# A linear attention and Fourier feed-forward kernel: its planned instruction order is kept for longer, with other priorities

## The chip, the cores and the metric

The kernel runs on one core of one Trainium2 chip. The metric is the device time of one execution in microseconds (us); less is better. The core's engines each work through a queue of their own, in order: PE (TensorE, matrix products), DVE (VectorE), ACT (ScalarE), POOL (GpSimd) and SP (SyncE, which mostly issues DMA transfers). Waits between engines go over semaphores.

## The reference

```python
# attention without softmax, per batch and head: q, k, v are (8, 8, 576, 64)
kv = np.einsum('bhsd,bhse->bhde', k, v)
out = np.einsum('bhsd,bhde->bhse', q, kv)
x = out / sqrt(mean(out**2, -1) + 1e-6) * g_norm      # then to (8, 576, 512)
# Fourier mixing and a feed-forward layer
u = x + real(fft(fft(x, axis=1), axis=2))
un = (u - mean(u)) / sqrt(var(u) + 1e-6)
y = u + maximum(un @ w_ch1, 0) @ w_ch2                # 512 -> 2048 -> 512
```

All arrays come in and go out in float32, the two weights in float64. For each of the 4608 tokens the feed-forward layer takes 2048 hidden values, in 16 slices of 128.

## The kernel before

**Stages.** For each batch of 576 tokens: `plan_kv` loads k and v and multiplies them (PE line 574); `plan_q_load` and `plan_q` load q and transpose it on PE (line 643, evicted by ACT at line 647); `plan_out` makes the attention output for three row groups t (PE line 669; ACT lines 686 and 691, DVE line 696 for the norm's sums, POOL line 709 for the gain); `plan_y` turns the sums into scales (ACT, DVE and POOL in turn); `plan_fold` scales and folds the rows into sums and differences (DVE lines 774 and 785, POOL lines 792 and 801, ACT line 798). Folding halves the Fourier transforms, which are products with cosine and sine tables: `plan_seq` along the tokens (PE line 816, ACT line 830, DVE line 834), `plan_chn` along the channels (PE line 851, ACT line 863, DVE line 871, sums on POOL at lines 883 and 886, then stores of u). `plan_turn` transposes u for the feed-forward layer (PE line 942, ACT line 951, DVE line 954). Large products are split into a high and a low part and take three passes.

The feed-forward layer works on nine blocks of 512 tokens. `plan_early` takes the first three of the 16 weight slices for a block as soon as its tokens are there: the first layer (PE line 424), the activation split on ACT and DVE (lines 434 and 437), the second layer (PE line 442), and partial sums stored to memory. `plan_w` converts float64 weights, mostly on DVE (lines 359 to 369, 986, 995). When all batches are through, a second part, written as a plain loop, does the other 13 slices.

**What sets the order in the first part.** The stages don't issue instructions at once. Each makes `Op` entries in a `Plan`, with an engine, a cost in nanoseconds, a rank (smaller goes first), the operations that it follows and the buffers it takes. `Plan.run` plays the entries through with these costs: at each simulated time an engine that is free takes, of the entries that are ready and whose buffers are free, the one of lowest rank, and only then are its instructions emitted. `rank(b, stage)` is 10 b + stage, with 40 less for batch 0; `KV, QT, OUT, SCL, FOLD, SEQ, CHN, NRM` are the stages 0 to 7; the evictions of `plan_out` have 20 less. `SHIFT` adds to the rank of a group of operations, named by stage, engine (or DMA) and rounded rank. Early feed-forward operations have ranks from 1000 on. `plan_spare` adds 45 operations of two matmuls each on a constant tile (line 494, cost 454) with the highest rank of all, ready from the plan's 12 us on: they fill time in which PE has nothing else to do, and are all emitted, so their number is fixed.

The emitted program then goes through a scheduler of the compiler, with a cost model of its own, which can reorder instructions of an engine where their dependencies allow it. `Plan.pin` keeps it from that: each instruction that is emitted up to `PIN_UNTIL` (in the plan's time, ns) gets a dependency without a semaphore on the one before it on its engine. `PINNED` lists all five engines.

```python
for i in traced[start:]:
    if i.engine not in self.pinned or now > PIN_UNTIL:
        continue
    last = self.last.get(i.engine)
```

Behind that limit the scheduler is free in its order. Matmuls on float32 operands show as two records each in the profile (lines 574 and 669): a k-v operation is 16 and 4 records, an output operation 32.

Of the kernel before, what the change touches and what calls it, by code (L numbers as in the profile page):

```python
# [46 lines left out]
SPARE_FROM = 12000  # L47


PIN_UNTIL = 95000  # L50
PINNED = {
    mybir.EngineType.PE, mybir.EngineType.DVE, mybir.EngineType.Activation,
    mybir.EngineType.Pool, mybir.EngineType.SP,
# [2 lines left out]


SHIFT = {
    ("", "POOL", 20): 18,
    ("chn", "ACT", -34): 54.5,  # L60
    ("dft", "DVE", -35): 83.5,
    ("fold", "DVE", -36): -33.5,
    ("out", "DVE", -58): 31,
    ("out", "ACT", 2): 157,
    ("q", "PE", -39): 3,
    ("q", "PE", 21): -30,
    ("q", "ACT", 31): -19.5,
    ("q_load", "DMA", -39): -1.5,
}


# [17 lines left out]
class Plan:  # L89
# [18 lines left out]
    def op(self, eng, cost, rank, emit, after=(), bufs=(), lag=0, port=False, wait=0):  # L108
        o = Op()
        o.port = port or eng == "POOL"  # L110
        o.dense = False
        o.wait = wait
        o.eng, o.cost, o.rank, o.emit, o.lag = eng, cost, rank, emit, lag
        o.after = [a for a in after if a is not None]
        o.bufs = list(dict.fromkeys(bufs))
        for b in o.bufs:
            b.left += 1
        o.n = len(self.ops)
        o.stage = emit.__qualname__.split("<locals>.")[1].split(".")[0]
        o.done, o.dma = None, False  # L120
        self.ops.append(o)
        return o
# [130 lines left out]
def kernel(  # L253
# [52 lines left out]
    op, dma = plan.op, plan.dma  # L306
# [165 lines left out]
    def rank(b, stage):  # L472
        return 10 * b + stage - (40 if b == 0 else 0)

    KV, QT, OUT, SCL, FOLD, SEQ, CHN, NRM = range(8)
# [25 lines left out]
    dft = {}  # L501
# [25 lines left out]
    def plan_kv(b):  # L527
        kvt = ring("kvt", qkv, [P, NPAIR, D], "kvt")
        ps = bank_buf("ps_k")
        mm, lds = [], []  # L530
        rest = []
        for c, src in (("k", k), ("v", v)):
            kr = Buf("kr", lambda c=c: qkv.tile([P // 2, H, D], F32, name=c + "r", tag="kr", bufs=RINGS["kr"]))
            rest.append(kr)
        for pr in range(NPAIR):
            hs = slice(2 * pr, 2 * pr + 2)
            ts = []
            ld = []
            for c, src, kr in (("k", k, rest[0]), ("v", v, rest[1])):
                on = dict(eng="ACT") if b == 0 and c == "v" else {}  # L540
                start = nc.scalar.dma_start if on else nc.sync.dma_start
                if b < 2 and pr >= NPAIR - EARLY_KV[b]:
                    main = Buf("h", lambda c=c: base.tile(
                        [P, 2, 4, D], F32, name=c + "m", tag="r", bufs=RINGS["h"]
                    ))
                else:
                    main = Buf("kv", lambda c=c: qkv.tile(
                        [P, 2, 4, D], F32, name=c + "m", tag="m", bufs=RINGS["kv"]
                    ))
                ts.append(main)  # L550
                ld.append(dma(
                    256, rank(b, KV),
                    lambda main=main, src=src, hs=hs, start=start: start(
                        main.t.rearrange("p h j d -> p h (j d)"),
                        src[b, hs, : 4 * P].rearrange("h (p j) d -> p h (j d)", j=4),
                    ),
                    bufs=[main], **on,
                ))
                if pr == 0:
                    lds.append(dma(  # L560
                        128, rank(b, KV),
                        lambda kr=kr, src=src, start=start: start(
                            kr.t, src[b, :, 4 * P :].rearrange("h p d -> p h d")
                        ),
                        bufs=[kr], **on,
                    ))

            def go(pr=pr, ts=ts):
                km, vm = ts[0].t, ts[1].t
                kr, vr = rest[0].t, rest[1].t  # L570
                for j in range(5):
                    for s in range(2):
                        h = 2 * pr + s
                        nc.tensor.matmul(  # L574
                            ps.t[s * D : (s + 1) * D, pr * D : (pr + 1) * D],
                            km[:, s, j, :] if j < 4 else kr[:, h, :],
                            vm[:, s, j, :] if j < 4 else vr[:, h, :],
                            start=(j == 0),
                            stop=(j == 4),
                        )  # L580

            mm.append(op("PE", 1080, rank(b, KV), go, ld + lds, [ps, kvt] + ts + rest))
        done = op(
            "ACT", 370, rank(b, KV),
            lambda: nc.scalar.copy(kvt.t.rearrange("p c t -> p (c t)"), ps.t[:, : NPAIR * D]),
            mm, [ps, kvt],
        )
        if b:
            return kvt, kvt, [done], ld

        kvg = ring("kvt", qkv, [P, NPAIR, D], "kvt")

        def gain():
            nc.vector.tensor_tensor(
                kvg.t, ps.t[:, : NPAIR * D].rearrange("p (c t) -> p c t", c=NPAIR),
                gb.unsqueeze(1).to_broadcast([P, NPAIR, D]), ALU.mult,
            )

        scaled = op("DVE", 330, rank(b, KV), gain, mm + [i_gb], [ps, kvg])
        return kvt, kvg, [done, scaled], ld  # L600
# [30 lines left out]
    def plan_q(b, side, j, qt, ld):  # L631

        n = TR + 1 if side == 0 and j == 0 else TR
        fq = ring("fq", qkv, [P, NPAIR, TR + 1], "fq")
        done = []
        ps = bank_buf("ps_q")

        def view():
            return ps.t[:, : NPAIR * n].rearrange("p (c t) -> p c t", c=NPAIR)

        def turn():
            for m in range(NPAIR):
                nc.tensor.transpose(view()[:, m, :], qt.t[:n, j, m * P : (m + 1) * P], ident[:n, :n])  # L643

        def take():
            dst = fq.t[:, :, :n]
            nc.scalar.copy(dst[:, :, TR - 1 :: -1] if side else dst, view())  # L647

        tr = op("PE", 330, rank(b, QT), turn, ld, [qt, ps, fq])
        done.append(op("ACT", 490, rank(b, QT), take, [tr], [ps, fq]))  # L650
        if side and j == 2:
            done.append(op(
                "POOL", 100, rank(b, QT), lambda: nc.gpsimd.memset(fq.t[:, :, TR:], 0.0), [tr], [fq]
            ))
        return fq, done
# [151 lines left out]
    def plan_seq(b, grp, xs, pt, dones):  # L807
        part, ch = divmod(grp, 2)
        ps = bank_buf("ps_f")

        def mm():
            idx = 0
            for t in range(3):
                n = rows[t]
                for a, c in passes:
                    nc.tensor.matmul(  # L816
                        ps.t[:, :NS],
                        xs[t].t[a][:n, part, ch * P : (ch + 1) * P],
                        cs[:n, part, c, t, :],
                        start=(idx == 0),  # L820
                        stop=(idx == 8),
                    )
                    idx += 1

        r = rank(b, SEQ)
        a = op("PE", 1200, r, mm, dones + [dft["s", part]], [ps, pt] + xs)
        a.dense = True
        h = op(
            "ACT", 414, r - D2,
            lambda: nc.scalar.activation(pt.t[0][:, part, ch, :], ps.t[:, :NS], AF.Copy), [a], [ps, pt],  # L830
        )

        def low():
            nc.vector.tensor_tensor(
                pt.t[1][:, part, ch, :], ps.t[:, :NS], pt.t[0][:, part, ch, :].bitcast(F32), ALU.subtract
            )

        return op("DVE", 450, r - D2, low, [h], [ps, pt])
# [78 lines left out]
    def plan_turn(b, side, t, x, done):  # L917
# [15 lines left out]
        ps = bank_buf("ps_t")  # L933
        blocks = [unTs[j] for j in dict.fromkeys(p[0] for p in pieces)]
# [7 lines left out]
                nc.tensor.transpose(view()[:, c, :], x.t[:n, at : at + P], ident[:n, :n])  # L942

        r = rank(b, NRM)
        a = op("PE", 330, r, turn, done, [x, ps] + blocks)
        for j, lo, hi, at, step in pieces:
            stop = at + step * (hi - lo - 1) + (1 if step > 0 else -1)
            to = slice(at, None if stop < 0 else stop, step)
# [121 lines left out]
    for b in range(B):  # L1070
        kvt, kvg, kvt_done, kv_loaded = plan_kv(b)
# [4 lines left out]
        xs = [ring("x", one, [P, 2 * DM], "x") for _ in range(3)]  # L1076
# [4 lines left out]
        for side in range(2):  # L1081
            qt, loaded = plan_q_load(b, side)
# [25 lines left out]
        pt = Buf("pt", lambda: [one.tile([P, 2, 2, NS], F32R, name=f"pt{i}") for i in range(2)])  # L1108
# [39 lines left out]
    r = rank(B, 5)  # L1148
    a = op("DVE", 300, r, p0_in, zeros)
    a = op("PE", 1200, r, p0_mm, [a], [ps0])  # L1150
    a = op("DVE", 900, r, p0_out, [a], [ps0, p0t, p0u])
# [86 lines left out]
    blocks = early[::-1][: len(early) - 2] + early[:2] + list(range(1, NBLK - NSEG)) + [0]  # L1238
# [198 lines left out]
```

## Time and profile before

| What | Value |
|---|---|
| Time, median of 3 runs | 1025.26 us (1024.71 to 1025.57) |
| Profiled execution, its own time | 1022.79 us |
| Its span | 1021.0 us |
| PE busy | 1002.3 us (98% of the span) |
| DVE, ACT, POOL busy | 475.3, 324.8, 314.4 us |

The span is the time from the first to the last instruction of the profiled execution, and the execution's own time is a little more. Rows of the profile name the line of the kernel, the engine, the operation and the tiles as `out<-in`; `x372` is the number of records. In rows of groups, busy us and mean ns follow, then the engine's idle time just before, with what ended it. In rows of stretches, the length comes first, then busy time and record count for PE, PEld (weight loads), DVE, ACT and POOL, then the granted TensorE clock (1.00 is full), the busy share of the DMA engines and GB/s. In a timeline, a start, a duration and an operation. Neighbouring matmuls overlap in the pipeline, so their durations exceed the distance between their starts.

### The profile page before, as it was taken

Reading aid. Unit: us, or ns where it says so; the run is one execution under the profiler, and the core shown is the slowest. Engines: PE = TensorE matmul, PEld = TensorE weight load, DVE = VectorE, ACT = ScalarE, POOL = GpSimd, SP = SyncE. Lnnn points to the kernel's source line nnn. Section 1 sums busy time; section 2 is a strip of 40 time slices with the busy share of each in tenths; the row PEclk is TensorE's granted clock in tenths of the full one; section 3 lists DMA queues with packets and bytes.
Section 4 is the critical chain, followed back from the end, with each engine's and each line's share of the span. In section 5 each row is a group of like instructions: output and inputs, shape, how many; then the busy total and the mean of one; then the engine's idle time right before and its main releaser. Section 6 shows DMA issues by size and latency. Waiting matters only on the chain.

```text
span 1021.0 us, 15425 instructions
## 1 busy us (share of the span) xinstructions
PE 1002.3 (98%) x6070; PEld 844.0 (83%) x6070; DVE 475.3 (47%) x847; ACT 324.8 (32%) x657; POOL 314.4 (31%) x328
## 2 busy tenths in 40 slices
PE   5999999999999999999999999999999999999997
PEld 5898888889888888888888888888888888888886
DVE  4897656654788879997131313131221311311211
ACT  2666556554644434344221202121121120210110
POOL 0526768775675132235722303020020010100000
PEclk9999999999999999999999999999999999999999
DMA  9989778664346775645553514230320400400101
GB/s 250 212 230 282 181 209 258 162 170 131 137 163 213 268 253 191 236 129 170 161 179 86 180 59 150 82 125 0 141 67 1 165 21 1 165 0 1 42 1 42
DMA packets 109260, 140.74 MB, mean 138 GB/s; under 512 B 51854, under 2 KB 76482, under 8 KB 104580
## 3 DMA queue, kind: packets, MB, share of 16 engines
q1 hardware_dynamic: 105652, 132.28, 41.9%
q0 software_dynamic: 1920, 6.29, 1.9%
q10 hardware_dynamic: 1616, 1.18, 0.5%
q8 instruction: 48, 0.79, 0.3%
q14 instruction: 24, 0.20, 0.1%
HBM read 88.33 MB, written 51.40 MB: 137 GB/s over the span
## 4 chain that ended last, share of the span: by engine, by line
PE 97%; DMA 1%; ACT 0%; POOL 0%; DVE 0%; issue 0%; SPq 0%; DVEq 0%; POOLq 0%
PE ps_h L424 38%; PE acc L442 38%; PE ps_o L669 4%; PE ps_f L816 4%; PE ps_f L851 4%; PE ps_k L574 3%; PE ps_s L494 2%; PE ps_q L643 2%; PE ps_t L942 2%; DMA qt<-in_q_dram 1%; PE ps_w L383 1%; DMA vm<-in_v_dram 0%; POOL x L883 0%; ACT x L686 0%; DVE uu L1324 0%
## 5 line engine op out<-in xcount | busy, mean ns | idle before, releaser
L424 PE MATMUL ps_h<-unTh,w 128*128 128x512 f32 x1152 | 356.6, 391 | 1.2 <-ACT fq L647 1.2
L442 PE MATMUL acc<-w,hh 128*128 128x512 f32 x1152 | 345.5, 390 | 0.0
L437 DVE SCALAR_TENSOR_TENSOR hl<-ps_h,hh 128x512 fp32r<-128x512 f32 x144 | 99.1, 688 | 371.8 <-ACT hh L434 367.5
L442 PEld LDWEIGHTS acc<-w,hh 128*128 128x128 f32 x1152 | 215.1, 188 | 44.3
L424 PEld LDWEIGHTS ps_h<-unTh,w 128*128 128x128 f32 x1152 | 214.8, 188 | 44.8 <-ACT fq L647 1.4
L434 ACT ACTIVATE hh<-ps_h 128x512 fp32r<-128x512 f32 x144 | 85.8, 596 | 454.0 <-PE ps_h L424 439.2
L424 PE MATMUL ps_h<-unTl,w 128*128 128x512 f32 x576 | 224.3, 389 | 0.0
L442 PE MATMUL acc<-w,hl 128*128 128x512 f32 x576 | 213.5, 389 | 0.0
L424 PEld LDWEIGHTS ps_h<-unTl,w 128*128 128x128 f32 x576 | 108.1, 188 | 22.6
L442 PEld LDWEIGHTS acc<-w,hl 128*128 128x128 f32 x576 | 108.1, 188 | 22.6
L1271 POOL DMA_INDIRECT uu<-u_scr,rowidx x24 | 23.2, 968 | 285.1 <-DVE uu L1324 177.9
L709 POOL TENSOR_TENSOR x<-x,gb 96x512 f32<-96x512 f32 (+1 forms) x42 | 55.0, 1330 | 45.7 <-ACT x L686 40.3
L1290 POOL TENSOR_TENSOR uu<-uu,up 128x512 f32<-128x512 f32 x36 | 45.7, 1298 | 45.2 <-ACT up L1287 45.2
L1234 POOL TENSOR_TENSOR w<-wap,w 128x512 fp32r<-128x512 f32 x18 | 26.4, 1467 | 75.3 <-ACT w L1233 69.1
L669 PEld LDWEIGHTS ps_o<-kvt,fq 64*96 64x96 f32 (+1 forms) x864 | 40.9, 162 | 5.7 <-issue 4.0
L1324 DVE SCALAR_TENSOR_TENSOR uu<-acc,rs_yb,uu 128x512 f32<-128x512 f32 x36 | 25.2, 744 | 42.5 <-PE acc L442 42.5
L669 PE MATMUL ps_o<-kvt,fq 64*96 64x64 f32 (+1 forms) x864 | 44.4, 248 | 0.0
L696 DVE TENSOR_REDUCE ss<-ps_o 96x8 f32<-96x512 f32 (+1 forms) x48 | 32.0, 682 | 26.5 <-ACT ps_o L691 26.3
L792 POOL TENSOR_TENSOR xe<-ab 96x256 f32<-96x256 f32 (+1 forms) x46 | 38.0, 845 | 18.7 <-DVE ab L785 17.9
L816 PE MATMUL ps_f<-cs,xh 96*128 96x290 f32 (+1 forms) x192 | 39.0, 300 | 0.0
L1278 DVE BATCH_NORM_STATS2 bst<-uu 128x6 f32<-128x512 f32 x36 | 24.5, 687 | 29.0 <-DMA uu<-u_scr,rowidx 19.8
L851 PE MATMUL ps_f<-cd,pt 128*96 128x258 f32 (+1 forms) x288 | 37.8, 285 | 0.0
(114 smaller groups left out, 1022.4 us busy)
## 6 DMA issues: line engine op xcount, KB each, us to landing
raw<-in_moe_w_ch_dram SPq DMA_DIRECT2D x32, 512.0 KB
unT_scr<-unTh SPq DMA_DIRECT2D x9, 1024.0 KB
unT_scr<-unTl SPq DMA_DIRECT2D x9, 1024.0 KB
part_scr<-part SPq DMA_DIRECT2D x36, 256.0 KB
unTh<-unT_scr SPq DMA_DIRECT2D x9, 1024.0 KB
unTl<-unT_scr SPq DMA_DIRECT2D x9, 1024.0 KB
up<-part_scr SPq DMA_DIRECT2D x36, 256.0 KB
out_dram<-uu SPq DMA_DIRECT2D x36, 256.0 KB
```

Of the source, the lines that this page charges most:

```text
L424: nc.tensor.matmul(ps, w[c][:, kc * P : (kc + 1) * P], unT[a][:, kc, :], start=(idx == 0), stop=(idx == 3 * KC - 1),)
L434: nc.scalar.activation(hh, ps, AF.Relu)
L437: nc.vector.scalar_tensor_tensor(hl, ps, 0.0, hh.bitcast(F32), ALU.max, ALU.subtract)
L442: nc.tensor.matmul(acc, hpair[a][:, i * P : (i + 1) * P], w[c], start=(first and n == 0), stop=(last and n == 2),)
L574: nc.tensor.matmul(ps.t[s * D : (s + 1) * D, pr * D : (pr + 1) * D], km[:, s, j, :] if j < 4 else kr[:, h, :], vm[:, s, j, :] if j < 4 els ...
L669: nc.tensor.matmul(pss[s].t[:n, at : at + D], fqs[side].t[half, m, :n], kvt.t[half, m], start=True, stop=True,)
L696: nc.vector.tensor_reduce(ss.t[0][:n, :, t, s::2], pss[s].t[:n].rearrange("p (u m e) -> p u m e", u=2, e=D), AX.X, ALU.add,)
L709: nc.gpsimd.tensor_tensor(v_, v_, gb[:n].unsqueeze(1).to_broadcast([n, H, D]), ALU.mult)
L792: nc.gpsimd.tensor_tensor(o[:, s], a[:, 0], a[:, 1], ALU.subtract if s else ALU.add)
L816: nc.tensor.matmul(ps.t[:, :NS], xs[t].t[a][:n, part, ch * P : (ch + 1) * P], cs[:n, part, c, t, :], start=(idx == 0), stop=(idx == 8),)
L851: nc.tensor.matmul(ps.t[:n, :ND], pt.t[a][:, part, ch, offs[t] : offs[t] + n], cd[:, part, c, ch, :], start=(idx == 0), stop=(idx == 5),)
L1290: nc.gpsimd.tensor_tensor(us[j][i], us[j][i], part, ALU.add)
```

## The change

The limit of the pin goes from the plan's 95 us to 260 us. The table of shifts is replaced: ten entries go, thirteen come. Four PE costs in the plan change. The new entries, by what they touch: the load of the token order; batch 3's stores of u, its norm sums on DVE and its gain on POOL; batch 2's fold on POOL; batch 0's loads of k and v, its query loads (two of the three row groups), its query copies on ACT and its output evictions on ACT; batch 4's output on PE; batch 2's query transposes on PE (to a lower rank, so earlier); the first weight slice on ACT and the third on DVE. The shifts that stood before are dropped where no new entry repeats them.

```diff
@@ -47,7 +47,7 @@
 SPARE_FROM = 12000
 
 
-PIN_UNTIL = 95000
+PIN_UNTIL = 260000
 PINNED = {
     mybir.EngineType.PE, mybir.EngineType.DVE, mybir.EngineType.Activation,
     mybir.EngineType.Pool, mybir.EngineType.SP,
@@ -56,16 +56,19 @@
 
 
 SHIFT = {
-    ("", "POOL", 20): 18,
-    ("chn", "ACT", -34): 54.5,
-    ("dft", "DVE", -35): 83.5,
-    ("fold", "DVE", -36): -33.5,
-    ("out", "DVE", -58): 31,
-    ("out", "ACT", 2): 157,
-    ("q", "PE", -39): 3,
-    ("q", "PE", 21): -30,
-    ("q", "ACT", 31): -19.5,
-    ("q_load", "DMA", -39): -1.5,
+    ("", "DMA", 20): 6,
+    ("chn", "DMA", 36): 166,
+    ("fold", "POOL", 24): 26.5,
+    ("kv", "DMA", -40): 3,
+    ("out", "ACT", -58): 54.5,
+    ("out", "DVE", 12): 169,
+    ("out", "POOL", 32): 53.5,
+    ("out", "PE", 42): 113.5,
+    ("q", "ACT", -39): 43,
+    ("q", "PE", 21): -38,
+    ("q_load", "DMA", -39): 7.5,
+    ("w", "ACT", -60): 43,
+    ("w", "DVE", 6): 158.5,
 }
 
 
@@ -579,7 +582,7 @@
                             stop=(j == 4),
                         )
 
-            mm.append(op("PE", 1080, rank(b, KV), go, ld + lds, [ps, kvt] + ts + rest))
+            mm.append(op("PE", 980, rank(b, KV), go, ld + lds, [ps, kvt] + ts + rest))
         done = op(
             "ACT", 370, rank(b, KV),
             lambda: nc.scalar.copy(kvt.t.rearrange("p c t -> p (c t)"), ps.t[:, : NPAIR * D]),
@@ -646,7 +649,7 @@
             dst = fq.t[:, :, :n]
             nc.scalar.copy(dst[:, :, TR - 1 :: -1] if side else dst, view())
 
-        tr = op("PE", 330, rank(b, QT), turn, ld, [qt, ps, fq])
+        tr = op("PE", 378, rank(b, QT), turn, ld, [qt, ps, fq])
         done.append(op("ACT", 490, rank(b, QT), take, [tr], [ps, fq]))
         if side and j == 2:
             done.append(op(
@@ -823,7 +826,7 @@
                     idx += 1
 
         r = rank(b, SEQ)
-        a = op("PE", 1200, r, mm, dones + [dft["s", part]], [ps, pt] + xs)
+        a = op("PE", 1250, r, mm, dones + [dft["s", part]], [ps, pt] + xs)
         a.dense = True
         h = op(
             "ACT", 414, r - D2,
@@ -942,7 +945,7 @@
                 nc.tensor.transpose(view()[:, c, :], x.t[:n, at : at + P], ident[:n, :n])
 
         r = rank(b, NRM)
-        a = op("PE", 330, r, turn, done, [x, ps] + blocks)
+        a = op("PE", 360, r, turn, done, [x, ps] + blocks)
         for j, lo, hi, at, step in pieces:
             stop = at + step * (hi - lo - 1) + (1 if step > 0 else -1)
             to = slice(at, None if stop < 0 else stop, step)
```

No other line changes: the instructions, their operands and the buffers are those of before.

## The prediction

> **What bounds the kernel now.** I read the page's first line, then a table of busy time by stretch, then the waits of PE (TensorE's matmul side), and last PE's timeline and its groups inside the stretch that the change touches.
>
> ```profile
> span 1021.0 us, 15425 instructions
> ```
>
> Busy time of each engine by stretch of the span (first columns: stretch, its length, PE busy):
>
> ```profile
> 0.00:25.00 25.00, 14.64 (x150) 12.33 (x152) 10.95 (x20) 6.05 (x11) 0.96 (x9) 1.00 1.06 250
> 25.00:95.00 70.00, 70.00 (x833) 60.10 (x831) 60.08 (x103) 42.07 (x93) 28.31 (x41) 1.00 0.93 242
> 95.00:225.00 130.00, 127.02 (x1335) 110.93 (x1332) 78.23 (x143) 77.12 (x180) 96.30 (x107) 1.00 0.76 203
> ...
> 260.00:330.00 70.00, 70.00 (x463) 61.35 (x462) 57.47 (x103) 37.98 (x85) 46.65 (x48) 1.00 0.46 161
> ```
>
> PE is busy for the whole of the second and the fourth stretch. It is the only engine that is: DVE, the next one, has 60.08 of 70 us and 57.47 of 70. The one place after the start where PE shows idle time is 95 to 225 us, 130 - 127.02 = 2.98 us. The granted clock is 1.00 in every row, so no row speaks of a slow TensorE. The kernel is a queue of PE work, and a new order can only save what PE loses between its instructions: open idle time, and matmuls that start later than they could while the row still counts PE as busy.
>
> At the start PE waits for its first load, and that is a row of the waits view:
>
> ```profile
> PE ps_q L643 <- DMA qt<-in_q_dram: 10.4, 1, 10.4
> ```
>
> **How large the loss is in 95 to 225 us.** A busy share of 98% hides late starts, so I price the work of that stretch by what the same work takes in the part that is pinned now. PE's timeline there (start, duration, operation; the distance between two starts is what a piece really took):
>
> ```profile
> 53.31 0.54 PE L816 MATMUL ps_f<-cs,xh 97*128 97x290 f32 x2
> ...
> 58.24 0.82 PE L643 MATMUL ps_q<-ident,qt 96*128 96x96 f32 x8
> ...
> 59.87 1.57 PE L669 MATMUL ps_o<-kvt,fq 64*96 64x64 f32 x32
> 61.37 4.55 PE L851 MATMUL ps_f<-cd,pt 128*97 128x258 f32 x36
> 65.76 0.82 PE L643 MATMUL ps_q<-ident,qt 96*128 96x96 f32 x8
> 66.52 0.69 PE L574 MATMUL ps_k<-vm,km 128*64 128x64 f32 x16
> 67.13 0.33 PE L574 MATMUL ps_k<-vr,kr 64*64 64x64 f32 x4
> 67.39 1.16 PE L383 MATMUL ps_w<-wa,mean_t 128*128 128x128 f32 x8
> 68.39 0.83 PE L942 MATMUL ps_t<-ident,x 97*128 97x97 f32 x8
> 69.15 0.69 PE L574 MATMUL ps_k<-vm,km 128*64 128x64 f32 x16
> ...
> 77.20 0.63 PE L424 MATMUL ps_h<-unTh,w 128*128 128x512 f32 x2
> ...
> 82.77 0.69 PE L574 MATMUL ps_k<-vm,km 128*64 128x64 f32 x16
> ...
> 115.26 0.57 PE L574 MATMUL ps_k<-vm,km 128*64 128x64 f32 x12
> 115.75 0.55 PE L942 MATMUL ps_t<-ident,x 97*128 97x97 f32 x4
> ...
> 120.94 0.88 PE L942 MATMUL ps_t<-ident,x 96*128 96x96 f32 x8
> ```
>
> In the pinned part operations are whole. A sequence transform (four groups of 9, line 816) takes 58.24 - 53.31 = 4.93 us, an attention output (line 669, 32 records) 1.50, a channel transform (line 851, 36 records) 4.39, two query transposes of four (line 643) 0.76, one k-v operation (line 574, 16 and 4 records) 0.87, two output transposes (line 942) 0.76, and two first-layer operations (line 424, 24 records between 77.20 and 82.77) 5.57. From 115.26 us they are not whole: a k-v operation breaks off after 12 of its 16 records, four transposes go between, and so on until 120.94. Those 5.68 us hold 15 rows with three k-v operations, three output transposes and two query transposes, which by the prices above take 3 x 0.87 + 5 x 0.38 = 4.51 us; 1.2 us is lost there.
>
> The work of the stretch, as the groups of PE between 95 and 225 us count it:
>
> ```profile
> L669 PE MATMUL ps_o<-kvt,fq 64*96 64x64 f32 (+1 forms) x372 | 20.3, 249 | 0.0
> L851 PE MATMUL ps_f<-cd,pt 128*96 128x258 f32 (+1 forms) x144 | 19.8, 288 | 0.0
> L816 PE MATMUL ps_f<-cs,xh 96*128 96x290 f32 (+1 forms) x96 | 19.7, 300 | 0.0
> L442 PE MATMUL acc<-w,hh 128*128 128x512 f32 x48 | 15.5, 403 | 0.0
> L424 PE MATMUL ps_h<-unTh,w 128*128 128x512 f32 x48 | 15.4, 402 | 1.2 <-ACT fq L647 1.2
> L574 PE MATMUL ps_k<-vm,km 128*64 128x64 f32 x288 | 14.5, 230 | 1.0 <-DMA vm<-in_v_dram 1.0
> ...
> L643 PE MATMUL ps_q<-ident,qt 96*128 96x96 f32 (+1 forms) x99 | 11.4, 250 | 0.3
> L942 PE MATMUL ps_t<-ident,x 96*128 96x96 f32 (+2 forms) x72 | 9.5, 254 | 0.4 <-POOL x L883 0.4
> ```
>
> Attention output 372 / 32 = 11.6 operations x 1.50 = 17.4; channel 144 / 36 = 4 x 4.39 = 17.6; sequence 96 / 24 = 4 x 4.93 = 19.7 (24 of the 36 records read xh); first layer 48 / 8 = 6 x 2.785 = 16.7; second layer 48 / 6 = 8 groups of 9 matmuls of the same size, at three quarters of 2.785, 16.7; k-v 288 / 16 = 18 x 0.87 = 15.7; query transposes 99 / 4 x 0.38 = 9.4; output transposes 18 x 0.38 = 6.8. The sum is 120.0 us in a stretch of 130. So 10.0 us is lost: 3.0 open idle time (ACT 1.2, a load of v 1.0, POOL 0.4, the rest small) and 7.0 in splits and late starts that the busy column hides. This is the ceiling of the change in this stretch.
>
> **The change, part by part.** No instruction of the computation is added or taken away. PE's work is the same to the record, the 45 filler operations of line 494 with it, since the plan only ends when all are emitted; a plan with less idle time moves them to later and doesn't drop them.
>
> *The pin to 260000.* Each engine's instructions now follow the plan up to its 260 us instead of its 95 us. The plan's clock isn't the trace's: the first split piece lies at 115.75 us, so the old limit falls at or shortly ahead of that, and the new one may fall near 280. The whole stretch in which PE loses time comes under it. Two terms follow. Splits and late starts, 7.0 us: an operation's matmuls follow one another, as in 25 to 95, so between nothing and all of it is recovered. Open idle time, 3.0 us: again between nothing and all, as the order decides. I take half of each, 3.5 + 1.5 = 5.0 us. All of it is what the pinned rows show (70.00 busy of 70), but those 70 us were cushioned by filler, whose row in the groups of 25 to 95 is
>
> ```profile
> L494 PE MATMUL ps_s<-still 128*128 128x512 f32 x64 | 18.2, 413 | 0.0
> ```
>
> and the later stretch has no such cushion, only first- and second-layer operations as the thing to do meanwhile. The middle is an estimate.
>
> *The price of pinning.* It adds dependencies only within an engine, and they cost nothing in themselves. What is queued behind a waiting instruction now waits too. On PE that is the next operation, even if its operands have lain ready; on ACT and DVE the evictions that free PSUM banks; on POOL the fold and output sums; on SP every load behind a store that waits for its data. Bounds: nothing, as in 25 to 95, up to the rival below. It is not added to the sum a second time, since half of the recovery is already withheld.
>
> *The thirteen priorities.* They change the order alone. Three touch the start: the first batch's query loads go from ahead of the k loads to behind them, apart from the two for the third row group; its query copies and weight clears on ACT drop behind others. PE's first wait is for a query load, and by the ranks a query load is still the first after the weight loads, so the 10.4 us stays; I cost it at nothing. Should the first batch's chain be slowed all the same, nothing covers it, because the filler is a fixed number; bounds 0 and +3.0 us, the open idle time that PE met in the later stretch when inputs came late. The conversion of the third weight slice on DVE drops behind the batches' own work; the early first-layer operations need it, and what hides its delay is filler until that is used up. Batch 3's norm reductions, its gain multiply and its stores, batch 4's attention output and batch 2's fold on POOL move later; what hides them is the other batches' work on the same engines, as PE's four full transforms in 130 us show. Half the gain withheld stands for these too. The filler itself may run in longer or shorter pieces: 18.2 / 64 = 0.284 us each against 2.785 / 12 = 0.232 in a long run, 90 records, at most 4.7 us less if all ran together, and none if they stay scattered; I take none.
>
> *The plan's costs* (k-v 1080 to 980, transposes 330 to 378 and 360, sequence 1200 to 1250). They shape the order only. The rows above have a k-v operation at 0.87 us, nearer the new 0.98 than the old 1.08, and a sequence operation at 4.93 / 4 = 1.23, near the new 1.25; for transposes 0.38 in a pair, the new figure for queries. I give the better costs no microseconds of their own.
>
> **The sum.** The profiled execution took 1022.79 us, its span 1021.0 and 1.79 around it. 1022.79 - 5.0 = 1017.8. The median of the runs shown is 2.47 us above the profiled execution, 1025.26, and the forecast is for that: 1025.26 - 5.0 = **1020.3 us**. With the whole 10.0 us it is 1015.3.
>
> **The rivals.** *First: a late input stops a full queue.* With the pin, PE stands at an operation whose input is late while ready work lies behind it. The place is the fold, which goes from DVE to POOL, ACT and POOL again before the sequence transform can start; POOL is busy 96.30 of 130 us in that stretch, its highest share, and a DMA load has already stopped PE there for 1.0. For it: the three waits on the rows above are of just this kind (ACT 1.2, DMA 1.0, POOL 0.4; mean 0.87). Against it: 25 to 95 runs pinned without one. Price: four and a half batches between 95 and 260, three folds each, 13 places x 0.87 = 11.3 us, less about 3.5 for splits that do go away: 1025.3 + 7.8 = 1033.1 us. It decides from about 6 such stops on, since 6 x 0.87 = 5.2 us uses up the 3.5 and 2 us more. The Trainium skill, TensorE: Matmul & The Clock Gate, section "Measured speedup vs the span model", says that matmuls run strictly in program order; by that rule nothing on PE softens a bad order, and the trace agrees, with PE idle 1.2 us at one first-layer matmul while later work stood queued. The same page, section "What's actually happening", has an idle time of about 3.4 us or more halve the clock until a window of work has passed; no wait after the start here is that long, and the granted clock stays 1.00.
>
> *Second: the gain is given back.* PE reaches 260 us sooner with the same DVE work behind it (57.47 of 70 us in 260 to 330), and then waits for weight conversions or evictions. That it is never idle there now, at 82% DVE, speaks against; that 5 us is a third of DVE's 12.5 us of free time speaks for. The time is 1025 us.
>
> *Third: the order hardly changes.* The scheduler may have kept nearly the plan's order anyway, and the splits be the smaller part of the 7.0, the rest being real late inputs that any order has. Then only the 1.2 us of the one split cluster goes: 1024 us.
>
> **How the numbers follow.** A measurement of this kernel can tell 0.2%, about 2 us, from no change. Forecast 0.57; stops 0.25; gain given back 0.11; order hardly changed 0.07. The forecast's own range is 1015.3 to 1023.2, which is all faster by over 2 us; the second and third rivals lie within 2 us. So faster 0.57, same 0.18, slower 0.25. The range goes from 1014.5, just under the full recovery, with a little of the filler's 4.7, to 1032; it holds the middle rivals and most of the first; left out are the worse half of the stops and a gain past the ceiling.
>
> **What would show it.** In the profile after: the filler's and the sums' record counts are the same; between 95 and 225 us k-v operations come as 16 and 4 records without transposes between; the same work by the prices above takes 120 to 127 us there; open idle time of PE after the start is under 2 us; the first wait stays at 10 to 11 us. The forecast is wrong if PE shows waits of 0.5 us and more for POOL, ACT or loads at the folds, adding up to over 6 us; if idle time appears ahead of the first first-layer operation; or if the saved time returns as waits for DVE between 260 and 400 us.

## The result, and the profile after

The changed kernel takes 1018.33 us in the median of 5 runs (1016.90 to 1019.72), the kernel before 1025.26 (1024.71 to 1027.99). The ratio is 0.9929, with a 95% interval of 0.9912 to 0.9946: 0.5 to 0.9% faster. The profiled execution took 1016.90 us with a span of 1015.1, against 1022.79 and 1021.0 before. The forecast was 1020.3 us in a range of 1014.5 to 1032.

The table of busy time by stretch, of the changed kernel (stretch, length, then busy time and records of PE, PEld, DVE, ACT, POOL, then the granted clock):

```profile
0.00:25.00 25.00, 12.83 (x144) 10.49 (x146) 11.05 (x20) 6.06 (x11) 0.96 (x9) 1.00 0.99 234
25.00:95.00 70.00, 69.59 (x835) 60.32 (x833) 60.93 (x102) 43.64 (x93) 28.61 (x40) 1.00 0.93 240
95.00:225.00 130.00, 130.00 (x1377) 115.40 (x1373) 79.86 (x148) 80.71 (x186) 97.92 (x110) 1.00 0.79 221
225.00:260.00 35.00, 33.85 (x280) 30.07 (x279) 18.28 (x35) 19.45 (x44) 22.03 (x24) 1.00 0.34 125
260.00:330.00 70.00, 70.00 (x443) 61.73 (x443) 56.18 (x106) 35.25 (x82) 41.46 (x45) 1.00 0.44 153
```

PE's open idle time between 95 and 225 us, 2.98 us before, is gone, and 42 more records pass in that stretch, 10 of them filler. The waits of PE in the whole span:

```profile
PE ps_q L646 <- DMA qt<-in_q_dram: 12.2, 1, 12.2
PE ps_o L672 <- ACT fq L650: 1.1, 1, 1.1
PE ps_q L646 <- issue: 0.4, 1, 0.4
```

The three waits of before behind the start have made room for one of 1.1 us, at 253 us. The first wait has grown from 10.4 to 12.2 us.

PE's groups between 95 and 225 us (lines are three further on than before; rows that aren't needed are left out):

```profile
L445 PE MATMUL acc<-w,hh 128*128 128x512 f32 x66 | 21.5, 406 | 0.0
L819 PE MATMUL ps_f<-cs,xh 96*128 96x290 f32 (+1 forms) x96 | 19.7, 300 | 0.0
L854 PE MATMUL ps_f<-cd,pt 128*96 128x258 f32 (+1 forms) x144 | 18.4, 283 | 0.0
L672 PE MATMUL ps_o<-kvt,fq 64*96 64x64 f32 (+1 forms) x352 | 17.4, 248 | 0.0
L427 PE MATMUL ps_h<-unTh,w 128*128 128x512 f32 x51 | 16.1, 395 | 0.0
...
L577 PE MATMUL ps_k<-vm,km 128*64 128x64 f32 x300 | 12.9, 228 | 0.0
L646 PE MATMUL ps_q<-ident,qt 96*128 96x96 f32 (+1 forms) x104 | 11.6, 249 | 0.0
...
L945 PE MATMUL ps_t<-ident,x 96*128 96x96 f32 (+2 forms) x72 | 7.9, 249 | 0.0
...
L497 PE MATMUL ps_s<-still 128*128 128x512 f32 x10 | 3.1, 410 | 0.0
```

At the prediction's prices this is 11 x 2.09 + 4 x 4.93 + 4 x 4.39 + 11 x 1.50 + 6.4 x 2.785 + 18.75 x 0.87 + 26 x 0.38 + 18 x 0.38 = 127.6 us of work in 130, and 10 filler records at 0.284 us take the other 2.8 (the last 0.4 is the error of the prices). Nothing else is lost. Why shows in the timeline: 15 rows for three k-v operations and five groups of transposes have become whole operations.

```profile
118.45 0.88 PE L945 MATMUL ps_t<-ident,x 97*128 97x97 f32 x8
119.26 0.69 PE L577 MATMUL ps_k<-vm,km 128*64 128x64 f32 x16
119.88 0.33 PE L577 MATMUL ps_k<-vr,kr 64*64 64x64 f32 x4
120.14 0.69 PE L577 MATMUL ps_k<-vm,km 128*64 128x64 f32 x16
120.76 0.33 PE L577 MATMUL ps_k<-vr,kr 64*64 64x64 f32 x4
121.02 0.88 PE L945 MATMUL ps_t<-ident,x 96*128 96x96 f32 x8
```

To set all runs side by side I use one figure, the **loss** of a stretch: its length less PE's records in it at those prices (for a part of an operation, its share; first- and second-layer matmuls at 2.785 / 12, and the few of lines 383 and 1131 at 0.11). Filler counts as loss and is given beside it, at 0.284 us each. All in us, of the profiled executions:

| Kernel | 0 to 95 us | 95 to 225 (filler in it) | 225 to 260 | 260 to 330 |
|---|---|---|---|---|
| before | 34.0 | 10.2 (0) | 0.3 | -0.9 |
| changed | 33.7 | 2.9 (2.8) | 0.9 | -0.3 |
| changed, a second execution | 34.2 | 2.8 (2.8) | 2.5 | -0.2 |

The 7.3 us between 95 and 225, less 0.6 and 0.6 behind them, come to 6.1 us, near the 5.9 us between the spans. So the first wait's 1.8 us is not lost within the first 95 us: less filler ran there, and its rest ran behind, where it takes the 2.8 us. The second execution shows how far one program's figures differ.

### The profile page after: what moved, and what is told of

Its sections match the earlier page's. It is cut to its first block, busy times and chain, and to the rows that moved or that the text cites. A ratio compares the mean times of both kernels' runs of the same rounds, so it can differ in the third digit from the quotient of the medians.

```text
span 1015.1 us, 15417 instructions
## 1 busy us (share of the span) xinstructions
PE 996.0 (98%) x6070; PEld 840.5 (83%) x6070; DVE 470.8 (46%) x847; ACT 328.2 (32%) x657; POOL 308.8 (30%) x328
## 4 chain that ended last, share of the span: by engine, by line
PE 98%; DMA 1%; ACT 0%; issue 0%; DVE 0%; SPq 0%; DVEq 0%; ACTq 0%
PE acc L445 39%; PE ps_h L427 39%; PE ps_o L672 4%; PE ps_f L819 4%; PE ps_f L854 3%; PE ps_k L577 3%; PE ps_s L497 2%; PE ps_q L646 2%; PE ps_t L945 2%; DMA qt<-in_q_dram 1%; PE ps_w L386 1%; DVE uu L1327 0%; PE ps_o L1134 0%; ACT x L689 0%; SPq L352 0%
## 5 line engine op out<-in xcount | busy, mean ns | idle before, releaser
L1237 POOL TENSOR_TENSOR w<-wap,w 128x512 fp32r<-128x512 f32 x18 | 23.2, 1291 | 70.4 <-ACT w L1236 70.4
```

## The experiments

The theory at the outset was that the pin does it, by keeping PE's operations whole. The rival was that the new priorities do it. Each run was set beside the kernel before on the same chip; ratios are to that, with 95% intervals.

**The pin alone.** On the kernel before:

```diff
-PIN_UNTIL = 95000
+PIN_UNTIL = 260000
```

> The kernel before with the pin's limit at 260 us and nothing else changed. Theory one (the pin does it, by keeping PE's operations whole): most of the 10 us lost between 95 and 225 us goes, the start stays at a first wait of 10.4 us, so 1016 to 1020 us. Theory two (the new priorities do it, and the old order pinned would stall): 1023 to 1030 us, with waits of PE of 0.5 us and more beyond 110 us that add up to 5 us or more.

Measured: 1016.22 us, ratio 0.9919 (0.9901 to 0.9938). The loss in 95 to 225 us is 2.0 (filler 0.6); PE's first wait is 10.2 us. One number, with the old order, brings as much as the whole change. The stretch's row:

```profile
95.00:225.00 130.00, 129.09 (x1369) 114.62 (x1368) 76.49 (x146) 81.25 (x187) 103.16 (x114) 1.00 0.81 217
```

The rival's stalls did not come: PE's waits behind the start add up to 2.1 us.

**The priorities and plan costs alone.** On the changed kernel:

```diff
-PIN_UNTIL = 260000
+PIN_UNTIL = 95000
```

> The changed kernel with the pin's limit back at 95 us; priorities and plan costs stay. Theory one (the pin): the splits and late starts return behind about 115 us, and the start's first wait is 12.2 us instead of 10.4, so 1024 to 1028 us. Theory two (the priorities): 1017 to 1021 us.

Measured: 1036.51 us, ratio 1.0120 (1.0097 to 1.0143), slower than either theory had it. Two waits of PE and a row of the stretches:

```profile
PE ps_k L577 <- DMA vm<-in_v_dram: 3.7, 2, 3.1
PE ps_f L819 <- POOL xl L804: 2.9, 1, 2.9
```

```profile
135.00:140.00 5.00, 5.00 (x34) 4.26 (x31) 0.00 (x0) 0.85 (x2) 2.93 (x5) 0.50 0.98 319
```

The loss in 95 to 225 us is 15.2 us. PE waited 3.1 us up to 134.7 us, and the granted clock of the next 5 us is 0.50. The rival falls; the theory missed that these priorities, with the new plan costs, do harm without the pin.

**The pin and the costs, with the old priorities.** The changed kernel with the ten entries of before in `SHIFT`.

> The changed kernel with the ten old priorities; pin and new plan costs stay. Theory one (the pin): as the pin alone, 1016 to 1020 us, the four costs being worth under 2 us either way. Rival (the corrected costs make the pinned order fit the chip): 3 us or more faster than the pin alone.

Measured: 1016.26 us, ratio 0.9916 (0.9897 to 0.9935), next to the pin alone. The loss in 95 to 225 us is 2.1. The costs are worth nothing that can be seen here.

**The first batch's loads in their old order.** On the changed kernel:

```diff
-    ("kv", "DMA", -40): 3,
-    ("q_load", "DMA", -39): 7.5,
+    ("q_load", "DMA", -39): -1.5,
```

> The changed kernel with the first batch's loads in the old order: its query loads ahead of its k and v loads. Theory one (the start cost 1.8 us and nothing covers it): the first wait goes from 12.2 back to 10.4 us and the time from 1018.3 to about 1016.5 us. Rival (the filler's fixed number covers it, since PE has nothing real to do there): the first wait is shorter and the time stays within 1 us of 1018.3, or rises because the later order was fitted to the later start.

Measured: 1034.87 us, ratio 1.0105 (1.0082 to 1.0127): neither. The first wait did shorten, to 10.7 us, but two entries of thirteen cost 16 us. The loss is 37.2 us by 95 us, then 6.4, 4.1 and 5.9. Behind the start, the longest wait of PE and the stretch after it are

```profile
PE ps_h L426 <- DVE w L997: 3.3, 1, 3.3
```

```profile
95.00:100.00 5.00, 4.34 (x15) 3.06 (x17) 3.13 (x4) 1.26 (x3) 4.29 (x5) 0.67 0.94 286
```

It is a first-layer operation that waits for the third weight slice, whose conversion the change had put behind the batches' work on DVE; here the filler had run out at 77.3 us (at 114.8 in the changed kernel).

**The changed kernel again,** beside the next three.

> The changed kernel once more, to stand beside the next three on one chip, and beside the pin alone (ratio 0.992 to the kernel before). Theory one (the pin does it, the priorities are worth nothing or cost a little by the later start): ratio 0.992 to 0.995, so 1017 to 1020 us. If the priorities help: under 0.990.

Measured: 1018.75 us, ratio 0.9950 (0.9931 to 0.9969). With the first measurement, the change is worth 0.3 to 0.9%. The pin alone and the pin with the costs are 2 us ahead in the medians, but the intervals touch; I don't call the priorities harmful on this. Nor is it shown that the later start is free: the kernels with a first wait of 9.8 to 10.2 us (these two, and the two at the end of this section) have ratios of 0.9912 to 0.9919, the changed kernel, with 12.2 us, 0.9929 and 0.9950.

**The pin on PE alone, and on all but PE.** The set `PINNED` of the changed kernel cut to PE, and without PE.

> The changed kernel with the pin (to 260 us) on PE alone; the other four engines are left to the scheduler. Theory one in its narrow form (whole operations on PE are the gain): 1017 to 1021 us. Rival (the order of the other queues, evictions, folds and loads, sets when PE's inputs come): PE waits of over 1 us appear, and the time is 1025 us or more.

> The changed kernel with the pin on the other four engines and PE left to the scheduler. Narrow theory (whole operations on PE): splits return, 6 to 10 us more than the changed kernel, 1024 to 1029 us. Rival (the other queues' order): within 2 us of the changed kernel.

Measured: 1035.35 us, ratio 1.0107 (1.0089 to 1.0124), and 1029.76, ratio 1.0055 (1.0034 to 1.0076). Both also took pins away from the first 95 us, which the kernel before had, and there much of the time went. The row of 25 to 95 us of the first and of the second:

```profile
25.00:95.00 70.00, 65.03 (x691) 55.72 (x688) 49.86 (x89) 36.10 (x79) 19.11 (x31) 0.93 0.83 214
```

```profile
25.00:95.00 70.00, 67.63 (x779) 59.36 (x778) 55.20 (x95) 37.59 (x82) 21.30 (x29) 0.95 0.75 198
```

PE is idle for 5.0 and 2.4 us there, and the clock is not full. By 95 us the loss is 43.5 and 45.2 us, against 34.2 in the changed kernel beside them. With the pin on PE alone, PE's records stand in the changed kernel's order, by tile and shape, up to 280 us, and it is still 16.6 us slower: what it loses, it loses to the other queues' order. How much of that is behind 95 us these two kernels can't say; two further ones below keep the pins of the first 95 us.

**The pin to the end of the first part.**

```diff
-PIN_UNTIL = 260000
+PIN_UNTIL = 1000000
```

> The changed kernel with the pin over the whole of the first part. Theory one: behind the plan's 260 us little is lost any more, since PE has early feed-forward work enough there and is idle for 1.1 us at most; within 1.5 us of the changed kernel. Rival (each further pinned stretch pays like 95 to 225 us did, 10 us in 130): 3 to 5 us faster. Second rival (a late input stops the full queue): slower by 3 us or more, with waits of PE behind 260 us.

Measured: 1022.61 us, ratio 0.9976 (0.9959 to 0.9993), 3.9 us more than the changed kernel beside it. Waits of PE that the changed kernel doesn't have:

```profile
PE ps_w L386 <- POOL wp L382: 1.0, 1, 1.0
PE ps_f L819 <- ACT xh L801: 0.9, 1, 0.9
PE ps_f L819 <- POOL xl L804: 0.8, 1, 0.8
PE ps_w L386 <- DVE wap L377: 0.5, 1, 0.5
```

The loss in 260 to 330 us is 2.9 us against -0.3. This is the prediction's first rival, a late input that stops a full queue, in the part where the pin was new. PE's own order is the changed kernel's up to 280 us by tile and shape; ACT, DVE and POOL leave it at 259 to 267 us. The longer pin also takes away something useful: two weight loads that the scheduler issues at 63 and 84 us in the changed kernel come at 262 us here. Whether the waits at line 386, which are for converted weights, follow from that was not tested.

**From 95 us on, PE alone pinned; and all but PE.** On the changed kernel, in `Plan.pin` (the second the other way round):

```diff
-            if i.engine not in self.pinned or now > PIN_UNTIL:
+            until = PIN_UNTIL if i.engine == mybir.EngineType.PE else 95000
+            if i.engine not in self.pinned or now > until:
```

> The changed kernel; all engines pinned to the plan's 95 us, from there to 260 us PE alone. Narrow theory (whole operations on PE are the gain): 1017 to 1021 us. Wider theory (the gain is that all queues follow one order; PE's order with other queues rearranged brings late inputs): 1024 to 1035 us, with the start to 95 us like the changed kernel's and waits of PE for ACT, DVE or POOL behind it.

> The changed kernel; all engines pinned to the plan's 95 us, from there to 260 us all but PE. Narrow theory: splits and late starts come back, 1024 to 1029 us. Wider theory: the splits alone cost 0.1 to 0.2 us each, a few us in all, 1020 to 1025 us, since the inputs still come in the plan's order.

Measured: 1028.18 us, ratio 1.0036 (1.0022 to 1.0051), and 1022.52, ratio 0.9979 (0.9965 to 0.9993). With PE alone pinned, its records stand in the changed kernel's order up to 280 us (the other queues leave theirs at 93 to 108 us), its operations are whole, and it waits, here in its row and its timeline (its lines are one further on):

```profile
95.00:225.00 130.00, 126.17 (x1324) 111.61 (x1323) 79.15 (x143) 75.58 (x178) 92.24 (x104) 0.99 0.72 209
```

```profile
109.28 0.40 PE L820 MATMUL ps_f<-cs,xl 96*128 96x290 f32 x1 [1.67 <-POOL xl L805]
...
127.26 0.72 PE L946 MATMUL ps_t<-ident,x 96*128 96x96 f32 x6 [0.39 <-POOL x L890]
...
150.33 0.74 PE L428 MATMUL ps_h<-unTh,w 128*128 128x512 f32 x2 [1.59 <-DVE ss L700]
```

With all but PE pinned, the other queues keep the changed kernel's order beyond 225 us and PE leaves it at 79 us. The open idle time is small, 0.54 us from 95 to 225, and the splits are back:

```profile
119.12 2.47 PE L673 MATMUL ps_o<-kvt,fq 64*96 64x64 f32 x32
121.53 0.55 PE L946 MATMUL ps_t<-ident,x 97*128 97x97 f32 x4
122.01 0.33 PE L578 MATMUL ps_k<-vm,km 128*64 128x64 f32 x2
122.27 0.55 PE L946 MATMUL ps_t<-ident,x 97*128 97x97 f32 x4
122.75 0.68 PE L578 MATMUL ps_k<-vm,km 128*64 128x64 f32 x14
```

The losses of 95 to 225 us without filler are 6.6 us with PE alone, 5.2 with all but PE, 0.1 with all (and 15.2 with none, in the run of the priorities alone). The narrow theory falls and the wider one stands: with these priorities the order has to be held on PE and on the other queues together. Which of the other four matters, and whether the old priorities behave alike, was not tested.

**The start's loads and the third weight back.** The run of 1034.87 us, less one more entry:

```diff
-    ("w", "DVE", 6): 158.5,
```

> The run with the first batch's loads in the old order (1034.9 us, ratio 1.0105), and the third weight slice's conversion on DVE at its old priority too. If that conversion's delay is what that run lost its time to (PE waited 3.3 us for it at 95 us): the wait is gone and the time is 1028 us or less, 6.6 us or more of the 16 back by the wait and the halved clock behind it. Rival (that order is bad at many places, and this wait is one of them): over 1030 us, with new waits.

Measured: 1015.39 us, ratio 0.9913 (0.9895 to 0.9931). The one entry is worth 19.5 us in that order. PE's first wait is 9.8 us, and behind it PE waits once, for 0.6 us. Its row:

```profile
95.00:225.00 130.00, 129.37 (x1356) 114.51 (x1355) 79.85 (x146) 77.97 (x179) 96.78 (x108) 1.00 0.80 222
```

The loss in 95 to 225 us is 1.4, and no filler is left by then. It is the lowest median of all, but its interval overlaps those of the pin alone and of the changed kernel's first measurement. The direct price of the wait, 3.3 us and some 5 us at a clock of 0.67, is under half of the 19.5; the waits near 230 and 300 us went too. How one entry at 80 us reaches those was not traced further than that the plan gives another order.

**Less filler.** The pin and costs with the old priorities, and `SPARE = 30` for 45. It leaves out a third of the matmuls on the constant tile, which no output uses.

> The pin and the new costs with the old priorities (1016.3 us, ratio 0.9916), with 30 filler operations instead of 45. If the filler's number is a fixed cost (0.5 us each): 7 us faster, 1009 to 1011 us. Rival (the filler only runs where PE has nothing to do): the same within 1.5 us, with PE's idle time up by about 7 us. Second rival (the idle time that replaces it halves the clock): slower by 3 us or more.

Measured: 1016.07 us, ratio 0.9912 (0.9890 to 0.9933), the same as with 45. PE's row of 25 to 95 us and its longest wait behind the start:

```profile
25.00:95.00 70.00, 67.03 (x837) 58.07 (x838) 59.14 (x104) 42.53 (x94) 28.36 (x42) 0.98 0.88 235
```

```profile
PE ps_w L383 <- DVE wa L986: 2.1, 1, 2.1
```

PE is idle for 3.0 us where it wasn't, the loss by 95 us falls by only 0.2 us, from 33.3 to 33.1, and 95 to 225 us loses 4.3 instead of 2.1. The filler's number is no cost here; it fills time that is lost either way. The second rival's clock did come (0.57 from 50 to 54 us, behind the wait of 2.1 us), but the time doesn't show it.

## Why the prediction was right, and where it was not

**The bound and the ceiling** held. PE's queue is what is shortened, and the stretch named, 95 to 225 us, is where the time came from. The price list gave 10.0 us of loss there; the changed kernel loses 2.9, of which 2.8 is filler.

**The term that was mis-sized** is the recovery. The prediction took half of it, 3.5 of 7.0 us of splits and late starts and 1.5 of 3.0 us of open idle time. Both went nearly whole: operations are unbroken, and PE is busy for 130.00 of 130 us. Of the table's 10.2, 7.3 show as net gain, because 2.8 us of filler moved in. The span's gain was 5.9 us and the medians' 6.9, against 5.0. The reason given for withholding half was that the later stretch lacks filler as a cushion. The pin alone, with 0.6 us of filler there, lost no more than 2.0 us, so the cushion wasn't needed.

**The mechanism** was put partly wrong. The prediction put the gain down to whole operations on PE and counted the pins on the other queues only as a risk. With these priorities, the stretch loses 15.2 us without the longer pin, 6.6 with PE alone pinned, 5.2 with all but PE, and 0.1 with all. So PE's own order is worth 5.1 to 8.6 us and the other queues' order 6.5 to 10.0, by which is added first: inputs that come in the order PE expects are at least as large a part as whole operations.

**The start** was called unchanged, on the ground that a query load is still the first after the weight loads. It isn't. SP's issues before (start, duration, transfer):

```profile
0.74 0.99 SPq L349 DMA_DIRECT2D raw<-in_moe_w_ch_dram  x2
1.77 0.43 SPq L610 DMA_DIRECT2D qt<-in_q_dram  x1
```

and in the changed kernel:

```profile
0.74 0.99 SPq L352 DMA_DIRECT2D raw<-in_moe_w_ch_dram  x2
1.77 0.43 SPq L486 DMA_DIRECT2D gb<-in_g_norm_dram  x1
2.25 3.29 SPq L613 DMA_DIRECT2D qt<-in_q_dram  x2
```

The old shift of -1.5 had put most of the first batch's query loads at ranks of -40.5 and -40.25, ahead of the gain vector's load at -40. With the new one they are at -31.5 and -31.25, the two unshifted ones at -38.5 lead, and the gain vector's load goes first. The first query load is issued 0.5 us later and the first wait grew by 1.8 us; where the rest comes from was not traced. With the old load order the wait was 10.7 and 9.8 us. It cost nothing by 95 us; whether it costs the 2 us by which the kernels with the earlier start are ahead stays open, inside the bound of 0 to +3.0.

**The first rival,** a late input in a full queue, did not happen in the changed kernel but is real: it shows with PE alone pinned, at the fold's last POOL step that the prediction named (1.67 us for `xl`), and with the pin to the end. **The second,** a gain given back to DVE behind 260 us, did not: PE is busy for 70.00 of 70 us. **The third,** an order hardly changed, did not.

**The priorities** were costed at nothing with half the gain withheld. That the sum came out within 2 us is in part luck: the gain withheld stood for harm from the priorities, which with the pin is about 2 us in the medians. That the table is so harmless could not be known from the working. With the new costs but without the longer pin it makes the kernel 12 us slower than before, and with the pin a table that differs in two entries is 16 us worse. The third weight's conversion was named as a risk that filler hides until it is used up, and that is just where the altered table lost first.

**The signs to look for** were right on the records (90 filler records, whole k-v operations) and on open idle time under 2 us behind the start (1.1 + 0.4), and wrong on the first wait, put at 10 to 11 us.

**Smaller slips.** The plan's clock runs closer to the trace's than assumed: the order of the kernel before and that of the pin alone part at 90 us on PE and at 94 to 102 us on ACT, DVE and POOL, ahead of 115.75 us, and by the run with the pin to the end the new limit falls near 260 us rather than 280. Of DVE's 12.5 us of free time 5 us is 0.4, not a third. The first rival's own price of 1033.1 us lies above the range's end of 1032. The clock of 1.00 in the row of 0 to 25 us doesn't fit the first matmuls: the eight of line 383 at 11.03 us take 1.80 us to the next start, and the same eight at 48.57 us take 0.85. What the prediction says of program order stands in the Trainium skill, TensorE: Matmul & The Clock Gate, section "The mechanism", one section ahead of the one that it names.

## What to carry to other kernels

Price the work of a stretch by what the same operations take where they run undisturbed; a PE that shows 98% busy hid more than twice its open idle time in broken operations and late starts (7.0 against 3.0 us). When a static order is held against a scheduler that would change it, hold it on every queue or expect late inputs, and find where to stop by trying it. A table of priorities is one piece: a part of it, tried on another order, says little about what that part is worth.

## What the hardware did that was not expected

Behind a short wait of PE the clock can be halved, and need not be. The changed kernel's wait of 1.15 us, up to 254.3 and 254.8 us, stands in both of its profiled executions. The stretch behind it, in the first and in the second:

```profile
256.00:260.00 4.00, 4.00 (x19) 3.32 (x18) 3.97 (x7) 2.81 (x6) 4.00 (x4) 1.00 0.17 66
```

```profile
256.00:260.00 4.00, 4.00 (x12) 3.13 (x11) 3.96 (x7) 2.49 (x6) 4.00 (x4) 0.57 0.01 2
```

The same program got a clock of 1.00 once and 0.57 the other time, and 19 matmul records through in 4 us or 12. The prediction had cited the Trainium skill, TensorE: Matmul & The Clock Gate, section "What's actually happening", by which it takes about 3.4 us of idle time to halve the clock, and had noted that no wait behind the start was that long. The measurement decides: the clock was halved behind a wait of 1.15 us in one execution of two. The run of the pin alone has half the clock behind a wait of 1.3 us too. Over the profiled executions of all kernels here, each of the seven waits of 2.1 to 3.3 us behind the start went with a halved clock, and five of the fourteen waits of 1.0 to 1.9 us did. What decides among the short ones was not traced.
